# Diagonal score groups taken two at a time, and score windows put in the order of their due times, in a gated-attention and maxout kernel

## The chip, the cores and the metric

One NeuronCore of a Trainium2 chip runs the whole kernel. The metric is the device time of one execution in microseconds (us); lower is better. The core's engines work side by side and wait for one another through semaphores: TensorE (PE; its weight loads are listed as PEld), VectorE (DVE), ScalarE (ACT), GpSimd (POOL) and SyncE (SP). SP and POOL are used here mainly as queues that issue DMA transfers. Matmul results go to PSUM, which has eight banks; everything else lives in SBUF.

## The reference

```python
# u, v: 8 x 3072 x 256, z: 8 x 3072 x 64
scale  = 1.0 / S                                   # S = 3072
scores = scale * np.matmul(z, z.transpose(0, 2, 1))
attn   = np.maximum(scores, 0.0) ** 2
x      = (u * np.matmul(attn, v)).reshape(B * S, D)
h1, h2 = x @ w1, x @ w2                            # 256 -> 1024
out    = np.maximum(h1, h2) @ w_out                # 1024 -> 256
```

Eight sequences of 3072 rows go through an attention without softmax: the scores are z times its own transpose, so the score matrix is symmetric, and each score goes through relu and a square. The result times v is gated by u and goes through a two-branch layer whose branches are joined by a maximum. The types at the interface are float32; the kernel computes in bfloat16 with float32 accumulation.

## The kernel before

**Tiling.** A sequence is cut into 24 blocks of 128 rows, and four blocks make a group (`G = 4`, 512 rows). One *step* produces the output of one group, so there are 6 steps per sequence and 48 in all. A step accumulates, over all 24 blocks `k`, the block of v times the 128 x 512 score tile of block `k` against the group, into two PSUM accumulators `xacc` (two halves of the 256 features; line 262, recorded at the helper's line 74). That makes 48 matmuls of 512 columns. At the step's end two DVE operations (line 268) gate it with u and give `xT`. Three steps later (`LAG = 3`) `xT` goes through the maxout layer: `chunk_d` (tiles `d_ps`, then `g_sb`) and `chunk_o` (tiles `o_ps`, then `o_sb`, then the store).

**Scores and their symmetry.** Since the score matrix is symmetric, each tile is computed once, on or above the diagonal, and used twice: as it is in its own step (tile `a_sb`), and transposed in a later step (tile `aT`, filled by a DMA transpose on SP's queue, `turn`, lines 200 and 226). A score needs only 64 features, so a score matmul uses only 64 rows of the 128 x 128 array: `score` (line 190) puts it on the lower half (`j = 0`) or the upper half (`j = 1`), and two matmuls on different halves run at the same time. `scores_pair` (line 204) does two blocks: two 512-column matmuls on the two halves, into one PSUM tile of two banks; ACT takes relu into `r_sb` (line 218), DVE squares it into `a_sb` (line 221), and SP transposes it where the other triangle needs it.

**The diagonal.** In the diagonal group of a step (4 x 4 blocks) only the upper triangle is computed: `scores_diag` (line 234) does 4, 3, 2 and 1 blocks, which are matmuls of 512, 384, 256 and 128 columns on the halves 0, 1, 1, 0. The first two go to one PSUM tile, the others to a second one. ACT takes the relu of the first (line 246, 896 columns), DVE that of the second (line 248, 384 columns), DVE squares the four rows into `aD` (lines 249 to 252), and three `turn`s fill the lower triangle of `aD`. The first four steps of the first sequence do without this (`NDIAG`): they compute their whole diagonal as pairs. So there are 44 diagonals.

**The order.** TensorE's order is written out by hand: `work` is the list of its pieces (one block of a step for both accumulators is 432 ns by the list's own account), and `matmul` pins each instruction in the order of the program (line 73). SP's and POOL's DMAs are pinned too; ACT and DVE are ordered by the compiler's scheduler. Score tiles are grouped in *windows*, and each window is put between two pieces of `work`: all its score matmuls stand there in a row. In `before`, `tiles` lists the tiles of all steps in the order of the steps, a diagonal first and then the pairs (lines 498 to 501), and `windows` cuts that list: up to three PSUM tiles per window (`WIN = 3`), where a diagonal counts as two (its second is the entry `-1`), so that a diagonal shares its window with one pair. The three PSUM tiles are all that `mm_psum` has; the scores share them with `d_ps` and `o_ps`.

Each row of scores has a due time: the time of its first reader in `work` less an allowance, 2900 ns for a row of the step's own (`LAT_OWN`), 9000 for a transposed one (`LAT_TURNED`), 10000 for a diagonal (`LAT_DIAG`). Windows are laid from the last to the first, each at the latest allowed place (`spots`) that is not after the due time of any of its rows and at least `GAP` (2500 ns) before the next window:

```python
    for w in reversed(range(len(windows))):
        limit = min([limit] + [due[r] for r in windows[w] if r in due])
        found = [i for i in spots if begins[i] <= limit]
        i = found[-1] if found else 0
        laid.setdefault(i, []).insert(0, w)
        limit = begins[i] - (GAP if w > n_first else GAP_FIRST)
```

A place is allowed where no `chunk_d` or `chunk_o` piece lies within 860 ns before it and 1700 after it, since those use the same PSUM tiles.

**Buffers.** `NA`, `NT`, `ND` (line 51) are the numbers of `a_sb`, `aT` and `aD` tiles. Loads of u, v and z go through POOL's queue, each behind a one-column copy (`gate`, line 83) of the tile last written (`fresh`), which holds the load back until that tile exists.

Of the kernel before, what the change touches and what calls it, by code (L numbers as in the profile page):

```python
# [11 lines left out]
def kernel(  # L12
# [17 lines left out]
    nc = tc.nc  # L30
    fp32 = mybir.dt.float32
    bf16 = mybir.dt.bfloat16
    AF = mybir.ActivationFunctionType
    ALU = mybir.AluOpType

    B, S, D = u.shape
# [3 lines left out]
    P = 128  # L40
    NSB = S // P
    G = 4
    WIN = 3
    GW = G * P
    NG = NSB // G
# [2 lines left out]
    LAG = 3  # L48
    NDIR = 3
    NDIAG = 3  # L50
    NA, NT, ND = 18, 12, 3
    scale = 1.0 / S
    c2 = float(scale * scale)

# [7 lines left out]
    apool = ctx.enter_context(tc.tile_pool(name="apool", bufs=NA))  # L62
    dpool = ctx.enter_context(tc.tile_pool(name="dpool", bufs=ND))
# [4 lines left out]
    mm_psum = ctx.enter_context(tc.tile_pool(name="mm_psum", bufs=3, space=bass.MemoryType.PSUM))  # L68
# [4 lines left out]
    def matmul(*args, **kw):  # L73
        pin(nc.tensor.matmul(*args, **kw))  # L74

    def sp_dma(**kw):
        pin(nc.sync.dma_start(**kw))
# [108 lines left out]
    def direct(b, i, j):  # L186
        return b == 0 and i < j <= NDIR


    def score(q, out_ps, j, k, s, q0, n):  # L190
        half = ds(j * dqk, dqk)
        matmul(
            out_ps,
            q.zT[half, k + 1 - j, :],
            q.zT[half, ds(G * s + 1 - j + q0, n), :],
            start=True,
            stop=True,
        )

    def turn(out_ap, in_ap):  # L200
        sp_dma(out=out_ap, in_=in_ap, transpose=True)


    def scores_pair(b, s, k0):
        q = seqs[b]
        s_ps = mm_psum.tile([P, 2, GW], fp32, name="s_ps", tag="mm")
        for j in range(2):
            score(q, s_ps[:, j, :], j, k0 + j, s, 0, G)
        yield
        a_sb = apool.tile([P, 2, GW], bf16, name="a_sb")  # L210
        r_sb = apool.tile([P, 2, GW], bf16, name="r_sb", bufs=3)

        head = b == 0 and s == 0 and k0 < 10
        keep = pin if head else lambda ins: None
        if head and k0 in (2, 6):
            keep(nc.vector.tensor_single_scalar(out=r_sb, in_=s_ps, scalar=0.0, op=ALU.max))  # L216
        else:
            keep(nc.scalar.activation(r_sb, s_ps, AF.Relu))  # L218
        if head and k0 < 4:
            yield  # L220
        keep(nc.vector.tensor_mul(a_sb, r_sb, r_sb))  # L221
        gj = k0 // G
        if gj > s and not direct(b, s, gj):
            if (s, gj) not in q.T:
                q.T[s, gj] = tpool.tile([P, G, G, P], bf16, name="aT")
            turn(
                q.T[s, gj][:, ds(k0 - G * gj, 2), :, :].rearrange("p k q x -> p (k q) x"),
                a_sb.rearrange("p j q -> p (j q)"),
            )
        yield a_sb  # L230

    def scores_diag(b, s):
        q = seqs[b]
        k = G * s
        s_ps = mm_psum.tile([P, 2 * G, P], fp32, name="s_ps", tag="mm")
        s2_ps = mm_psum.tile([P, 2 * G, P], fp32, name="s2_ps", tag="mm")
        score(q, s_ps[:, 0:4, :], 0, k, s, 0, 4)
        score(q, s_ps[:, 4:7, :], 1, k + 1, s, 1, 3)  # L240
        score(q, s2_ps[:, 2:4, :], 1, k + 2, s, 2, 2)
        score(q, s2_ps[:, 4:5, :], 0, k + 3, s, 3, 1)
        yield
        aD = dpool.tile([P, G, G, P], bf16, name="aD")
        r_sb = apool.tile([P, 7, P], bf16, name="r_sb", bufs=3)
        nc.scalar.activation(r_sb, s_ps[:, 0:7, :], AF.Relu)  # L246
        r2_sb = apool.tile([P, 3, P], bf16, name="r2_sb", bufs=2)
        nc.vector.tensor_single_scalar(out=r2_sb, in_=s2_ps[:, 2:5, :], scalar=0.0, op=ALU.max)  # L248
        nc.vector.tensor_mul(aD[:, 0, :, :], r_sb[:, 0:4, :], r_sb[:, 0:4, :])
        nc.vector.tensor_mul(aD[:, 1, 1:4, :], r_sb[:, 4:7, :], r_sb[:, 4:7, :])  # L250
        nc.vector.tensor_mul(aD[:, 2, 2:4, :], r2_sb[:, 0:2, :], r2_sb[:, 0:2, :])
        nc.vector.tensor_mul(aD[:, 3, 3, :], r2_sb[:, 2, :], r2_sb[:, 2, :])
        for r in range(G - 1):
            turn(
                aD[:, r + 1 : G, r, :],
                aD[:, r, r + 1 : G, :].rearrange("p q x -> p (q x)"),
            )
        yield aD

    def attn(q, k, moving, xacc, dcs, first, last):  # L260
        for dc in dcs:
# [68 lines left out]
    q = seqs[0]  # L330
# [21 lines left out]
    fresh = [None]  # L352
# [61 lines left out]
    steps = [Step(b, s) for b in range(B) for s in range(NG)]  # L414
# [26 lines left out]
    for n, st in enumerate(steps):  # L441
        b, s = st.b, st.s
# [52 lines left out]
    put_o(last, True)  # L495


    tiles = []
    for n, st in enumerate(steps):
        for k0 in st.rows:  # L500
            tiles += [(n, None), (n, -1)] if k0 is None else [(n, k0)]
    windows, room = [], 0
    for i, (n, k0) in enumerate(tiles):
        if not room or (k0 is None and room < 2):
            windows.append([])
            room = 2 if i < 6 else WIN
        windows[-1].append((n, k0))
        room = 0 if (n + 1) % NG == 0 and k0 == -1 else room - 1

    begins, t = [], 0  # L510
    for ns, _, _, _ in work:
# [2 lines left out]
    due = {}  # L514
    for at, (_, _, _, reads) in zip(begins, work):
        for row, lat in reads if reads != "begin" else ():
            due[row] = min(due.get(row, t), at - lat)
    shared = [(at, at + w[0]) for at, w in zip(begins, work) if w[1]]

    def free(at):  # L520
# [13 lines left out]
        if free(at) and apart(at) and work[i][1] is False and work[i][0]  # L534
    ]
    GAP_FIRST, GAP = 2100, 2500
    n_first = sum(n < NG for n, _ in tiles) // WIN
    laid = {}
    limit = t
    for w in reversed(range(len(windows))):  # L540
# [3 lines that stand above are left out]
# [33 lines left out]
    for n, st in enumerate(steps):  # L577
        b, s = st.b, st.s
# [21 lines left out]
    transfers.sort()  # L600

    def scores_window(w):
        gens = []
        for n, k0 in windows[w]:
            st = steps[n]
            if k0 is None:
                gens.insert(0, (st, k0, scores_diag(st.b, st.s)))
            elif k0 >= 0:
                gens.append((st, k0, scores_pair(st.b, st.s, k0)))
        for st, k0, gen in gens:  # L610
            next(gen)
        for st, k0, gen in gens:
            st.scored[k0] = a = next(gen)
            fresh[0] = a[:, 0, 0:1] if k0 is not None else a[:, 0, 0, 0:1]


    steps[0].begin()
# [14 lines left out]
    gens = [scores_pair(0, 0, k0) for _, k0 in windows[0]]  # L632
# [12 lines left out]
    for i, (_, _, fn, _) in enumerate(work):  # L645
        for w in laid.get(i, []):
            scores_window(w)
        while transfers and transfers[0][0] <= begins[i]:
            _, _, is_load, begin_transfer = transfers.pop(0)
            if is_load:  # L650
                gate(fresh[0])
            begin_transfer()
        fn()
# [30 lines left out]
```

## Time and profile before

| what | value |
|---|---|
| median of 3 runs | 981.85 us (981.44 to 981.95) |
| the profiled execution, its own time | 981.29 us |
| span of the profiled execution | 979.5 us |
| granted TensorE clock | 1.00 over the span |
| PE matmuls on s_ps (scores) | 696 rows: 564 of 512 columns, 44 each of 384, 256 and 128 |
| mean of such a row | 380, 333, 269 and 216 ns |
| matmul rows on xacc, 512 columns | 379 ns |
| ACT relu, 1024 columns (L218) / 896 columns (L246) | 258 of 1023 ns / 44 of 917 ns |
| DVE relu of the diagonal's rest, 384 columns (L248) | 44 of 558 ns |
| DVE square of a pair, 1024 columns (L221) | 260 of 691 ns |
| DVE squares of a diagonal (L249 to L252) | 44 each of 425, 350, 292 and 218 ns |
| SP transposes aD / aT | 132 / 228, of 1.21 / 1.28 us each on the queue |
| the same, from issue to landing (lowest, median, longest) | 2.3, 2.4, 8.0 us / 3.1, 3.6, 10.6 us |
| DMA engines | hardware queue 61.5%, software queue 21.6% of 16 engines' span |

The profile's page gives, for the span of one execution, the busy time of each engine, the same in 40 equal slices (a digit is the busy share of a slice in tenths), and the chain of work that ended last, followed back from the last instruction. A line of a timeline has start, duration, engine, line of the code, operation, tiles (written <- read), shape and count; several equal instructions are drawn as one line. A line of the waits has the engine and tile that waited, what ended the wait, the total in us, how often, and the longest. A matmul's drawn duration is longer than the distance to the next matmul's start, because matmuls are pipelined: distances between starts tell what one costs. Some matmul records are missing in the trace, so counts on a matmul line can be a little short.

### The profile page before, as it was taken

Reading aid. Unit: us, or ns where it says so; the run is one execution under the profiler, and the core shown is the slowest. Engines: PE = TensorE matmul, PEld = TensorE weight load, DVE = VectorE, ACT = ScalarE, POOL = GpSimd, SP = SyncE. Lnnn points to the kernel's source line nnn. Section 1 sums busy time; section 2 is a strip of 40 time slices with the busy share of each in tenths; the row PEclk is TensorE's granted clock in tenths of the full one; section 3 lists DMA queues with packets and bytes.
Section 4 is the critical chain, followed back from the end, with each engine's and each line's share of the span. In section 5 each row is a group of like instructions: output and inputs, shape, how many; then the busy total and the mean of one; then the engine's idle time right before and its main releaser. Section 6 shows DMA issues by size and latency. Waiting matters only on the chain.

```text
span 979.5 us, 14514 instructions
## 1 busy us (share of the span) xinstructions
PE 968.7 (99%) x5662; PEld 510.3 (52%) x5743; DVE 432.2 (44%) x681; ACT 442.6 (45%) x500; POOL 77.7 (8%) x228
## 2 busy tenths in 40 slices
PE   9999999999999999999999999999999999999998
PEld 3355545555455554555545564455545555445556
DVE  6654444443544435433445334444345443554322
ACT  6853454334643355433554335533355433654322
POOL 2011000110001100010000100011000110000000
PEclk9999999999999999999999999999999999999999
DMA  9999599987999969897788979889778796796621
GB/s 151 171 161 187 103 182 150 164 149 123 175 160 144 155 123 177 150 170 128 151 156 144 179 119 157 148 153 181 135 147 149 136 187 127 149 161 118 109 66 65
DMA packets 378517, 143.46 MB, mean 146 GB/s; under 512 B 356944, under 2 KB 358608, under 8 KB 378448
## 3 DMA queue, kind: packets, MB, share of 16 engines
q1 hardware_dynamic: 361888, 112.78, 61.5%
q0 software_dynamic: 16560, 29.74, 21.6%
q8 instruction: 45, 0.74, 0.3%
q14 instruction: 24, 0.20, 0.1%
HBM read 59.77 MB, written 25.17 MB: 87 GB/s over the span
## 4 chain that ended last, share of the span: by engine, by line
PE 99%; issue 1%; DVE 0%; ACT 0%
PE xacc L74 52%; PE o_ps L74 21%; PE d_ps L74 17%; PE s_ps L74 8%; PE w2o_ps L74 0%; ACT r_sb L218 0%; DVE r_sb L216 0%; PE tpz L134 0%; DVE a_sb L221 0%; DVE o_sb L317 0%; DVE blank L333 0%
## 5 line engine op out<-in xcount | busy, mean ns | idle before, releaser
L74 PEld LDWEIGHTS <-v_sb 128*128 128x128 bf16 x2304 | 215.9, 98 | 277.7 <-issue 41.1
L218 ACT ACTIVATE r_sb<-s_ps 128x1024 bf16<-128x1024 f32 x258 | 248.6, 1023 | 111.4 <-PE s_ps L74 111.2
L221 DVE TENSOR_TENSOR a_sb<-r_sb 128x1024 bf16<-128x1024 bf16 x260 | 179.4, 691 | 212.9 <-ACT r_sb L218 208.9
L74 PE MATMUL xacc<-a_sb,v_sb 128*128 128x512 bf16 x997 | 231.3, 379 | 2.5 <-issue 0.2
L74 PE MATMUL xacc<-aT,v_sb 128*128 128x512 bf16 x912 | 216.5, 379 | 0.0
L74 PE MATMUL o_ps<-w_out_sb,g_sb 128*128 128x256 bf16 x1536 | 199.1, 273 | 0.0
L74 PE MATMUL d_ps<-xT,w_sb 128*128 128x512 bf16 x751 | 172.7, 379 | 0.9
L74 PEld LDWEIGHTS <-g_sb 128*128 128x128 bf16 x1536 | 149.9, 98 | 27.6
L292 ACT ACTIVATE g_sb<-d_ps 128x1024 bf16<-128x1024 f32 x96 | 98.3, 1024 | 138.8 <-PE d_ps L74 138.8
L292 DVE TENSOR_SCALAR g_sb<-d_ps 128x1024 bf16<-128x1024 f32 x96 | 117.4, 1223 | 84.7 <-PE d_ps L74 81.3
L323 ACT COPY o_sb<-o_ps 128x512 f32<-128x512 f32 x94 | 55.1, 586 | 178.2 <-PE o_ps L74 178.2
L268 DVE SCALAR_TENSOR_TENSOR xT<-xacc,uT 128x512 bf16<-128x512 f32 x96 | 62.0, 683 | 137.4 <-PE xacc L74 137.4
L74 PEld LDWEIGHTS <-w_sb 128*128 128x128 bf16 x768 | 75.1, 98 | 88.7
L74 PE MATMUL s_ps<-zT 64*128 64x512 bf16 (+3 forms) x696 | 89.2, 359 | 0.1
L246 ACT ACTIVATE r_sb<-s_ps 128x896 bf16<-128x896 f32 x44 | 40.3, 917 | 97.9 <-PE s_ps L74 97.9
L74 PE MATMUL xacc<-aD,v_sb 128*128 128x512 bf16 x331 | 79.9, 379 | 2.6 <-issue 2.2
L74 PE MATMUL o_ps<-W2o_sb,xT 128*128 128x256 bf16 x384 | 73.3, 273 | 0.0
L248 DVE TENSOR_SCALAR r_sb<-s_ps 128x384 bf16<-128x384 f32 x44 | 24.6, 558 | 95.3 <-PE s_ps L74 95.3
L74 PEld LDWEIGHTS <-zT 64*128 64x128 bf16 x696 | 27.3, 94 | 62.6 <-issue 50.5
L83 POOL COPY gate_sb<-g_sb 128x1 bf16<-128x1 bf16 x44 | 8.3, 188 | 407.8 <-DVE g_sb L292 238.5
L74 PEld LDWEIGHTS <-xT 128*128 128x128 bf16 x384 | 37.6, 98 | 4.3
L83 POOL COPY gate_sb<-a_sb 128x1 bf16<-128x1 bf16 x48 | 9.7, 202 | 271.8 <-DVE a_sb L221 271.8
(37 smaller groups left out, 143.3 us busy)
## 6 DMA issues: line engine op xcount, KB each, us to landing
out_dram<-o_sb SPq DMA_DIRECT2D x47, 512.0 KB, 4.1
v_sb<-in_v_dram POOLq DMA_DIRECT2D x48, 256.0 KB, 5.9
u_sb<-in_u_dram POOLq DMA_DIRECT2D x48, 256.0 KB, 5.3
aT<-a_sb SPq DMA_TRANSPOSE x228, 3.6
z_sb<-in_z_dram POOLq DMA_DIRECT2D x7, 384.0 KB, 7.5
aD<-aD SPq DMA_TRANSPOSE x132, 2.4
w_sb<-in_moe_w_dram POOLq DMA_DIRECT2D x2, 512.0 KB, 7.5
uT<-u_sb SPq DMA_TRANSPOSE x48, 4.3
```

The costliest lines, as they stand in the source:

```text
L74: pin(nc.tensor.matmul(*args, **kw))
L83: pin(nc.gpsimd.tensor_copy(gate_sb, tile_ap))
L218: keep(nc.scalar.activation(r_sb, s_ps, AF.Relu))
L221: keep(nc.vector.tensor_mul(a_sb, r_sb, r_sb))
L246: nc.scalar.activation(r_sb, s_ps[:, 0:7, :], AF.Relu)
L248: nc.vector.tensor_single_scalar(out=r2_sb, in_=s2_ps[:, 2:5, :], scalar=0.0, op=ALU.max)
L268: nc.vector.scalar_tensor_tensor(out=xT[:, dc, :].rearrange("p (t q) -> p t q", q=P), in0=xacc[dc].rearrange("p (t q) -> p t q", q=P), sca ...
L292: nc.any.tensor_single_scalar(out=g_sb[:, nb : nb + 2, :], in_=d_ps, scalar=0.0, op=ALU.max)
L323: nc.any.tensor_copy(o_sb[:, ds(2 * th, 2), :], o_ps[:, :, :D])
```

## The change

Two diagonals of neighbouring steps become one window, in three PSUM tiles instead of four: each has a tile for its rows of 4, 3 and 1 blocks (512, 384 and 128 columns on the halves 0, 1, 1; eight blocks, so the tile is full), and the two rows of 2 blocks share the third tile, one on each half and in a bank each. ACT takes the relu of each full tile (1024 columns), DVE that of the shared one in one operation (512 columns). A diagonal no longer stands with a pair.

The list of windows is made anew for each sequence: pairs in threes (the first six of the kernel in twos), diagonals in twos, and then all windows of the sequence are sorted by the earliest due time of their rows. The buffers become 13 `a_sb` (from 18), 13 `aT` (from 12) and 4 `aD` (from 3).

```diff
-    NA, NT, ND = 18, 12, 3
+    NA, NT, ND = 13, 13, 4
...
-    def scores_diag(b, s):
+    def scores_diags(b, ss):
         q = seqs[b]
-        k = G * s
-        s_ps = mm_psum.tile([P, 2 * G, P], fp32, name="s_ps", tag="mm")
-        s2_ps = mm_psum.tile([P, 2 * G, P], fp32, name="s2_ps", tag="mm")
-        score(q, s_ps[:, 0:4, :], 0, k, s, 0, 4)
-        score(q, s_ps[:, 4:7, :], 1, k + 1, s, 1, 3)
-        score(q, s2_ps[:, 2:4, :], 1, k + 2, s, 2, 2)
-        score(q, s2_ps[:, 4:5, :], 0, k + 3, s, 3, 1)
+        one = [mm_psum.tile([P, 2 * G, P], fp32, name="s_ps", tag="mm") for _ in ss]
+        two = mm_psum.tile([P, 2, G, P], fp32, name="s2_ps", tag="mm")
+        for s, s_ps in zip(ss, one):
+            k = G * s
+            score(q, s_ps[:, 0:4, :], 0, k, s, 0, 4)
+            score(q, s_ps[:, 4:7, :], 1, k + 1, s, 1, 3)
+            score(q, s_ps[:, 7:8, :], 1, k + 3, s, 3, 1)
+        for h, s in enumerate(ss):
+            score(q, two[:, h, 0:2, :], h, G * s + 2, s, 2, 2)
         yield
-        aD = dpool.tile([P, G, G, P], bf16, name="aD")
-        r_sb = apool.tile([P, 7, P], bf16, name="r_sb", bufs=3)
-        nc.scalar.activation(r_sb, s_ps[:, 0:7, :], AF.Relu)
-        r2_sb = apool.tile([P, 3, P], bf16, name="r2_sb", bufs=2)
-        nc.vector.tensor_single_scalar(out=r2_sb, in_=s2_ps[:, 2:5, :], scalar=0.0, op=ALU.max)
...
+        aDs = [dpool.tile([P, G, G, P], bf16, name="aD") for _ in ss]
+        r2_sb = apool.tile([P, 2, 2, P], bf16, name="r2_sb", bufs=2)
+        for h, s_ps in enumerate(one):
+            aD = aDs[h]
+            r_sb = apool.tile([P, 2 * G, P], bf16, name="r_sb", bufs=3)
+            nc.scalar.activation(r_sb, s_ps, AF.Relu)
+            if h == 0:
+                nc.vector.tensor_single_scalar(
+                    out=r2_sb, in_=two[:, :, 0:2, :], scalar=0.0, op=ALU.max
+                )
+            nc.vector.tensor_mul(aD[:, 0, :, :], r_sb[:, 0:4, :], r_sb[:, 0:4, :])
+            nc.vector.tensor_mul(aD[:, 1, 1:4, :], r_sb[:, 4:7, :], r_sb[:, 4:7, :])
+            nc.vector.tensor_mul(aD[:, 2, 2:4, :], r2_sb[:, h], r2_sb[:, h])
+            nc.vector.tensor_mul(aD[:, 3, 3, :], r_sb[:, 7, :], r_sb[:, 7, :])
+            for r in range(G - 1):
+                turn(
...
+        yield aDs
...
-    tiles = []
-    for n, st in enumerate(steps):
-        for k0 in st.rows:
-            tiles += [(n, None), (n, -1)] if k0 is None else [(n, k0)]
-    windows, room = [], 0
-    for i, (n, k0) in enumerate(tiles):
-        if not room or (k0 is None and room < 2):
-            windows.append([])
-            room = 2 if i < 6 else WIN
-        windows[-1].append((n, k0))
-        room = 0 if (n + 1) % NG == 0 and k0 == -1 else room - 1
...
+    windows = []
+    for b in range(B):
+        mine = [NG * b + s for s in range(NG)]
+        tiles = [(n, k0) for n in mine for k0 in steps[n].rows if k0 is not None]
+        part = [tiles[i : i + 2] for i in range(0, 6, 2)] if b == 0 else []
+        tiles = tiles[sum(map(len, part)) :]
+        part += [tiles[i : i + WIN] for i in range(0, len(tiles), WIN)]
+        diags = [n for n in mine if steps[n].diag]
+        part += [[(n, None) for n in diags[i : i + 2]] for i in range(0, len(diags), 2)]
+        windows += sorted(part, key=lambda w: min(due[r] for r in w))
...
     def scores_window(w):
-        gens = []
-        for n, k0 in windows[w]:
-            st = steps[n]
-            if k0 is None:
-                gens.insert(0, (st, k0, scores_diag(st.b, st.s)))
-            elif k0 >= 0:
-                gens.append((st, k0, scores_pair(st.b, st.s, k0)))
+        rows = windows[w]
+        b = steps[rows[0][0]].b
+        if rows[0][1] is None:
+            gen = scores_diags(b, [steps[n].s for n, _ in rows])
+            next(gen)
+            for (n, _), a in zip(rows, next(gen)):
+                steps[n].scored[None] = a
+                fresh[0] = a[:, 0, 0, 0:1]
+            return
+        gens = [(steps[n], k0, scores_pair(b, steps[n].s, k0)) for n, k0 in rows]
```

More of the change, by code (lines that the diff above doesn't have):

```diff
@@ L230, in scores_pair @@
         yield a_sb
-    def scores_diag(b, s):
+    def scores_diags(b, ss):
         q = seqs[b]
-        k = G * s
-        s_ps = mm_psum.tile([P, 2 * G, P], fp32, name="s_ps", tag="mm")
-        s2_ps = mm_psum.tile([P, 2 * G, P], fp32, name="s2_ps", tag="mm")
-        score(q, s_ps[:, 0:4, :], 0, k, s, 0, 4)
-        score(q, s_ps[:, 4:7, :], 1, k + 1, s, 1, 3)
-        score(q, s2_ps[:, 2:4, :], 1, k + 2, s, 2, 2)
-        score(q, s2_ps[:, 4:5, :], 0, k + 3, s, 3, 1)
-        yield
-        aD = dpool.tile([P, G, G, P], bf16, name="aD")
-        r_sb = apool.tile([P, 7, P], bf16, name="r_sb", bufs=3)
-        nc.scalar.activation(r_sb, s_ps[:, 0:7, :], AF.Relu)
-        r2_sb = apool.tile([P, 3, P], bf16, name="r2_sb", bufs=2)
-        nc.vector.tensor_single_scalar(out=r2_sb, in_=s2_ps[:, 2:5, :], scalar=0.0, op=ALU.max)
[L249 to L258, printed above, removed]
@@ new lines, in scores_diags @@
+        aDs = [dpool.tile([P, G, G, P], bf16, name="aD") for _ in ss]
[14 more added lines that the diff above has]
+                turn(
+                    aD[:, r + 1 : G, r, :],
+                    aD[:, r, r + 1 : G, :].rearrange("p q x -> p (q x)"),
+                )
@@ L536 @@
     GAP_FIRST, GAP = 2100, 2500
-    n_first = sum(n < NG for n, _ in tiles) // WIN
+    n_first = sum(w[0][0] < NG for w in windows)
     laid = {}
@@ L613, in scores_window @@
             st.scored[k0] = a = next(gen)
-            fresh[0] = a[:, 0, 0:1] if k0 is not None else a[:, 0, 0, 0:1]
+            fresh[0] = a[:, 0, 0:1]
     steps[0].begin()
```

## The prediction

> **What bounds the kernel now.** I read the page first: engine totals, slices, and the chain that ended last.
>
> ```profile
> span 979.5 us, 14514 instructions
> PE 968.7 (99%) x5662; PEld 510.3 (52%) x5743; DVE 432.2 (44%) x681; ACT 442.6 (45%) x500; POOL 77.7 (8%) x228
> ...
> PE   9999999999999999999999999999999999999998
> ...
> PE 99%; issue 1%; DVE 0%; ACT 0%
> ```
>
> TensorE is busy in every slice and the chain of waits never leaves it. A busy row does not yet exclude pauses under 1%, so I next read the waits of PE:
>
> ```profile
> PEld L74 <- issue: 92.7, 244, 0.4
> ...
> PE xacc L74 <- issue: 2.4, 15, 0.2
> ```
>
> After the start-up, PE waits for no engine and no DMA. What is left is "issue", at most 0.4 us at a time, and the timeline shows what that is:
>
> ```profile
> 23.74 2.76 PE L74 MATMUL xacc<-a_sb,v_sb 128*128 128x512 bf16 x12
> 26.43 0.82 PE L74 MATMUL s_ps<-zT 64*128 64x512 bf16 x6
> 27.19 2.76 PE L74 MATMUL xacc<-a_sb,v_sb 128*128 128x512 bf16 x12
> 29.88 0.82 PE L74 MATMUL s_ps<-zT 64*128 64x512 bf16 x6
> ```
>
> Twelve 512-column matmuls in 2.76 us, the last drawn 0.379 long, start (2.76 - 0.379)/11 = 0.216 us apart. From 23.74 to 26.43 are 2.69 us: eleven steps of 0.216 and one of 0.312. So going from the full array to the two half-array (64-row) score matmuls costs 0.096 us. The last score pair of a window starts 0.308 us before the next full matmul (single starts in the trace), 0.092 over its own 0.216: the way back. **Every score window therefore costs PE two turnovers, 0.188 us, besides its columns.** The window with a diagonal:
>
> ```profile
> 77.74 1.03 PE L74 MATMUL xacc<-aT,v_sb 128*128 128x512 bf16 x4
> 78.70 0.66 PE L74 MATMUL s_ps<-zT 64*128 64x512 bf16 x6
> 79.29 0.60 PE L74 MATMUL xacc<-aT,v_sb 128*128 128x512 bf16 x2
> ```
>
> Its six matmuls are 512, 384, 256, 128 columns of a diagonal and 512, 512 of a pair; single starts in the trace are 78.701, .704, .877, .927, .983, .986, then 79.294. The three kinds of window, from first score matmul to next full matmul plus 0.096: three pairs 0.754 + 0.096 = 0.850 (70 of them), diagonal and pair 0.594 + 0.096 = 0.690 (44), two pairs 0.538 + 0.096 = 0.634 (3). Together 59.50 + 30.36 + 1.90 = 91.76 us.
>
> **The change on PE.** The instruction order of the changed program has 110 runs of score matmuls where 117 stood: 84 of three pairs, 4 of two, 22 of two diagonals (512, 384, 128, 512, 384, 128, 256, 256). The number of matmuls, their columns and all others are the same. Call the lower half A (512, 512, 256) and the upper B (384, 128, 384, 128, 256). Gaps from the trace: 384 columns to the next on the same half 0.173; 128 columns to the next 0.056; 512 to the next 0.226 the first time in a window, 0.216 then; starts keep the program's order. A512 at 0; B384 0.003; B128 0.176; A512 0.226; B384 at 0.176 + 0.056 = 0.232; B128 0.163 to 0.173 after it, 0.395 to 0.405; A256 0.442; B256 between 0.445 (A sets it) and 0.461 (B sets it). Then its 256 columns (0.109) and the way back (0.092): 0.646 to 0.662. I take 0.652, with the turnover in 0.748.
>
> Sum: 84 x 0.850 + 22 x 0.748 + 4 x 0.634 = 71.40 + 16.46 + 2.54 = 90.39. **Change -1.37 us**, with the two ends of the new window -1.50 and -1.15. Nearly all is seven windows fewer at 0.188 (1.32 us); the packing of the columns itself gives next to nothing.
>
> A rule speaks against it. The Trainium skill, "TensorE: Matmul & The Clock Gate", Part 3, says that a weight load overlaps running matmuls only when it goes to another row group. The row first: 384 columns and then 256 on the same half started 0.173 apart, 0.162 being the 384 columns alone, so that load was covered here. By the rule half B would go as in the third rival below, and the sum would be +6.6 instead of -1.37. The row decides.
>
> **The other engines, costed at nothing.** ACT: 44 activations grow from 917 to 1023 ns, +4.7 us on an engine busy 45%. DVE: 44 of 558 ns become 22 of 512 columns, by the line from 384 (558) to 1024 (1222) some 691 ns: 24.6 falls to 15.2 us. The multiplies are the same (425, 350, 292, 218). DMA: the same 132 aD and 228 aT transposes, reordered. The cover of all this is the lead that a window has over its first reader. For pairs:
>
> ```profile
> 300.59 0.82 PE L74 MATMUL s_ps<-zT 64*128 64x512 bf16 x6
> ...
> 301.02 2.85 ACT L218 ACTIVATE r_sb<-s_ps 128x1024 bf16<-128x1024 f32 x3 [2.76 <-PE s_ps L74]
> ...
> 302.08 0.69 DVE L221 TENSOR_TENSOR a_sb<-r_sb 128x1024 bf16<-128x1024 bf16 x1 [2.75 <-ACT r_sb L218]
> ...
> 303.91 0.69 DVE L221 TENSOR_TENSOR a_sb<-r_sb 128x1024 bf16<-128x1024 bf16 x1 [0.23 <-ACT r_sb L218]
> ```
>
> The first pair is ready 2.18 us after the window's start, the third 4.01. The planner puts a window 2.9 us ahead of its first own row (LAT_OWN), and rows in due order are read 0.86 us per pair: third 2.9 + 1.73 - 4.01 = 0.6 us spare, which is positive without help from other slack. In the trace of before the smallest steady spare was 0.42 (at 150.7). Should ACT be held by one g_sb of 1.02 us, 0.4 us would show on PE, once. Turned tiles (aT) landed at least 12.8 us before their first matmul, so the queue's new order has that to spend. a_sb buffers fall from 18 to 13: at one window of three pairs per 3.45 us, the densest stretch (above), a buffer is wanted again after 13/3 x 3.45 = 14.9 us, while its multiply ends 4 us after the window's start at the latest and its transpose landed within 10.6 (3.6 in the median). PSUM: a new window takes three tiles as one of three pairs does, and gives them back sooner (two activations and one DVE operation, not three activations in line). If any of these runs out, its engine's next PSUM eviction is late, then a score window on PE.
>
> **Where the new order could bite: the diagonal of step 4 in each sequence.** Before:
>
> ```profile
> 198.52 0.66 PE L74 MATMUL s_ps<-zT 64*128 64x512 bf16 x6
> ...
> 200.35 3.74 SPq L77 DMA_TRANSPOSE aD<-aD  x3
> ...
> 205.55 3.87 SPq L77 DMA_TRANSPOSE aD<-aD  x3
> ...
> 211.10 1.89 PE L74 MATMUL xacc<-aD,v_sb 128*128 128x512 bf16 x8
> ```
>
> The turns go out 1.83 us after the window's start, 1.26 apart; the third landed at 205.26, 5.6 us before the weight load of the first reader (210.87). Now the window stands two pieces of 0.43 later (199.38), its ACT row is 0.11 longer: first turn near 201.3, third near 203.85. Two windows in front of the reader (2 x 0.690) become one (0.748): the reader comes at 210.24. Behind these three turns SP now holds three of step 5, wanted a step later (979.5/48 = 20.4 us), and then the output store (issued at 210.86 before). POOL's next loads are gated by the window's last tile, as before (204.79 then, near 205 now). Turns landed in 2.3 to 8.0 us, median 2.4: at 2.4 the reader has 4.0 us to spare, at 6.56 (the turn of 205.55) it is 0.2 late, at 8.0 1.6 late. I take the median, to which most rows are near.
>
> **Sum.** The profiled execution took 981.29 (span 979.5), so 979.9 for one like it; it lies 0.56 under the median of the three runs, 981.85. Against that median: 980.5 us. My case's own range is 979.9 (981.44 - 1.50) to 980.8 (981.95 - 1.15).
>
> **Rivals.**
> Late turns, slower: at step 4's diagonal of seven sequences the third turn falls into the v loads issued at 205.38 and 206.02 and lands after 8.0 us. Price 7 x 1.6 = 11.2 - 1.4: 991.7; it beats the gain by 0.2% from 0.5 us late in each, a turn of 6.9 us or more. For: the turn at 205.55 took 6.56. Against: the new third turn goes out 1.5 us before that load, and the aT turn issued at 204.20 landed in 3.1. Chance 0.11.
> More gain, faster: the idle of the weight loads ("issue" 41.1 us before v_sb and 50.5 before zT) is what windows really cost, 91.6/117 = 0.78 each; seven fewer give 5.5: 976.4. Against: start-to-start gaps account for the period of 3.45 us with 0.188. Scatter of the runs with the upper end of my gain also counts here. Chance 0.12.
> Half B in line with its own weight loads, so that the packed window is dearer (slower too): a zT load (94 ns in the page's row) after the columns at each of B's four successions puts B256 at 0.003 + 2 x (0.162 + 0.094) + 2 x (0.056 + 0.094) = 0.815 instead of 0.451, 0.364 longer; 22 x 0.364 - 1.4 = +6.6: 988.5. Against: the 0.173 above. Chance 0.03.
> That the change does less than it says (order alone, no packing: each 512 waits for the one before and nothing of B hides, 0.662) is the upper end of my own case.
>
> **Chances.** My case 0.74. A measurement of this kernel tells about 0.2% (1.96 us) from no change; my gain of 0.14% lies inside. Within: 0.69 of my case and 0.01 of late turns, 0.70. Faster: 0.05 of mine by scatter and 0.12, 0.17. Slower: 0.10 and 0.03, 0.13. Range 979.5 (the low end with 0.4 of scatter) to 982.5 (the turns 0.3 us late in each of seven), which leaves out about 2 in 10.
>
> **What would show it.** 110 score windows; windows of eight matmuls lasting 0.65 us to the next full matmul; no wait of PE for DVE, ACT or DMA beyond the first 20 us; a span near 978.2; ACT busy some 5 us more, DVE some 9 less. I am wrong if PE shows waits on aD transposes, or if the gap between the second B384 and its B128 exceeds 0.2 us.

## The result, and the profile after

The changed kernel took 988.46 us in the median of 14 executions (981.03 to 1000.02); the kernel before, run beside it, took 981.92 (981.44 to 993.08, 14 executions). The ratio is 1.0051 (95% interval 1.0026 to 1.0076; executions more than 1.5% above the fastest of their kernel are left out of ratios, which therefore understate the loss, while the medians and counts given here take all). The change made the kernel slower, by 0.5% in that ratio and 6.5 us in the medians, where 980.5 and "the same" had been predicted.

The distribution tells more than the median. The fastest execution, 981.03, is below every one of before beside it, and it is the one that was profiled; but 13 of 14 lie above 983 us. So the profile shows the gain and only the beginning of the loss. Its page, engine totals and chain of waits:

```profile
span 979.3 us, 14613 instructions
PE 968.0 (99%) x5662; PEld 510.8 (52%) x5743; DVE 416.3 (43%) x659; ACT 446.6 (46%) x500; POOL 77.9 (8%) x228
...
PE 97%; DMA 1%; issue 1%; DVE 0%; ACT 0%
PE xacc L74 51%; PE o_ps L74 21%; PE d_ps L74 17%; PE s_ps L74 8%; DMA aD<-aD 1%; PE w2o_ps L74 0%; ACT r_sb L218 0%; DVE r_sb L216 0%; PE tpz L134 0%; ACT r_sb L252 0%; DVE aD L257 0%; DVE a_sb L221 0%; DVE aD L258 0%; DVE o_sb L325 0%; DVE aD L259 0%
```

The second line of the chain, shares by line, has an entry that before did not have: DMA aD, the transposes of the diagonal. The waits of PE and of its weight loads name it too (who waited, what ended it, total us, times, longest):

```profile
PE xacc L74 <- DMA aD<-aD: 0.4, 1, 0.4
...
PEld L74 <- DMA aD<-aD: 1.2, 2, 0.9
```

It is a small wait, at one place, in step 4 of the seventh sequence. In the timeline of after:

```profile
802.39 8.12 SPq L77 DMA_TRANSPOSE aD<-aD  x6
...
803.44 0.19 POOL L83 COPY gate_sb<-aD 128x1 bf16<-128x1 bf16 x1 [3.08 <-DVE aD L257]
...
803.89 0.53 POOL L86 DMA_DIRECT2D v_sb<-in_v_dram  x1 [0.26 <-issue]
...
804.53 0.53 POOL L86 DMA_DIRECT2D v_sb<-in_v_dram  x1
...
812.96 1.04 PE L74 MATMUL xacc<-aD,v_sb 128*128 128x512 bf16 x4 [0.42 <-DMA aD<-aD]
```

The three turns that the reader needs went out at 802.39, 803.75 and 805.04 and landed at 809.14, 812.91 and 813.27: 6.8 to 9.2 us each, where the median of all aD turns is 2.4. Two v loads of 256 KB were issued between them and landed at 811.43 and 812.73. That is the place and the mechanism of the prediction's rival "late turns".

**The spare time of the step-4 turns** (from the landing of the last of the three to the weight load of the first matmul that reads the tile; the block that the third turn fills is read only 1.3 us later, so a spare just below zero need not show as a wait) was, in the seven steady sequences of the two profiled executions:

| | 2nd | 3rd | 4th | 5th | 6th | 7th | 8th |
|---|---|---|---|---|---|---|---|
| before, us | 5.62 | 3.30 | 5.68 | 5.01 | 5.59 | 5.02 | 5.63 |
| after, us | 1.43 | -0.53 | 1.28 | 0.89 | 1.64 | -1.97 | 4.04 |

From the second sequence on every other aD tile had at least 13 us in after, and PE waited for no aT tile; in the first sequence the tile of step 4 had 3.4 us, where it had 3.1 before. The eighth has no later sequence to load for, and there the 4.0 us that the prediction worked out are what was measured.

How the loads moved is read from the second sequence. After:

```profile
202.16 7.69 SPq L77 DMA_TRANSPOSE aD<-aD  x6
...
203.21 0.19 POOL L83 COPY gate_sb<-aD 128x1 bf16<-128x1 bf16 x1 [3.08 <-DVE aD L257]
...
203.66 0.53 POOL L86 DMA_DIRECT2D v_sb<-in_v_dram  x1 [0.26 <-issue]
```

and before:

```profile
200.35 3.74 SPq L77 DMA_TRANSPOSE aD<-aD  x3
...
204.93 0.19 POOL L83 COPY gate_sb<-a_sb 128x1 bf16<-128x1 bf16 x1 [5.64 <-DVE a_sb L221]
...
205.38 0.53 POOL L86 DMA_DIRECT2D v_sb<-in_v_dram  x1 [0.26 <-issue]
```

Before, the load's gate copied the pair's `a_sb`, written last in the window, 4.6 us after the first turn went out. In after a diagonal window has no pair. The tile that gates is the first square of the second diagonal (`fresh` takes `a[:, 0, 0, 0:1]`), 1.05 us after the first turn. The turns went out 1.8 us later than before and the loads 1.7 us earlier: they now start in the middle of the turns.

Something else changed that the prediction had not looked at, the stretch ahead of the turns. Busy time by stretches of 10 us; the last two columns are the busy share of the DMA engines (which can exceed 1) and GB/s. Before, then after:

```profile
170.00:180.00 10.00, 9.95 (x49) 4.39 (x49) 6.02 (x10) 3.88 (x4) 1.16 (x4) 1.00 0.70 127
180.00:190.00 10.00, 9.95 (x68) 6.19 (x68) 2.08 (x3) 4.03 (x5) 1.64 (x5) 1.00 1.12 165
190.00:200.00 10.00, 10.00 (x51) 4.40 (x50) 4.69 (x7) 3.10 (x4) 1.44 (x4) 1.00 1.15 214
```

```profile
170.00:180.00 10.00, 9.95 (x50) 4.22 (x49) 5.61 (x7) 4.90 (x5) 0.70 (x2) 1.00 1.19 208
180.00:190.00 10.00, 9.95 (x69) 6.21 (x69) 2.08 (x3) 4.03 (x5) 2.10 (x7) 1.00 1.19 172
190.00:200.00 10.00, 10.00 (x48) 4.48 (x46) 3.74 (x4) 2.05 (x2) 1.31 (x4) 1.00 1.18 237
```

Before had a lull (0.70) before the diagonal's turns; after has none. Pairs cut in threes put two pairs of step 4 into one window with the last of step 3, and the whole window takes the earliest due time of its rows. Their two aT turns, issued at 204.20 and 209.51 before, go out at 187.34 and 188.68 now: between 165 and 192 us SP issues nine aT turns where it issued four.

### The profile page after: what moved, and what is told of

Same layout as the page of the kernel before. It is cut to its first block, busy times and chain, and to the rows that moved or that the text cites. A ratio compares the mean times of both kernels' runs of the same rounds, so it can differ in the third digit from the quotient of the medians.

```text
span 979.3 us, 14613 instructions
## 1 busy us (share of the span) xinstructions
PE 968.0 (99%) x5662; PEld 510.8 (52%) x5743; DVE 416.3 (43%) x659; ACT 446.6 (46%) x500; POOL 77.9 (8%) x228
## 4 chain that ended last, share of the span: by engine, by line
PE 97%; DMA 1%; issue 1%; DVE 0%; ACT 0%
PE xacc L74 51%; PE o_ps L74 21%; PE d_ps L74 17%; PE s_ps L74 8%; DMA aD<-aD 1%; PE w2o_ps L74 0%; ACT r_sb L218 0%; DVE r_sb L216 0%; PE tpz L134 0%; ACT r_sb L252 0%; DVE aD L257 0%; DVE a_sb L221 0%; DVE aD L258 0%; DVE o_sb L325 0%; DVE aD L259 0%
## 5 line engine op out<-in xcount | busy, mean ns | idle before, releaser
L218 ACT ACTIVATE r_sb<-s_ps 128x1024 bf16<-128x1024 f32 x258 | 245.8, 1024 | 162.4 <-PE s_ps L74 162.2
L300 ACT ACTIVATE g_sb<-d_ps 128x1024 bf16<-128x1024 f32 x96 | 98.3, 1024 | 133.3 <-PE d_ps L74 133.3
L252 ACT ACTIVATE r_sb<-s_ps 128x1024 bf16<-128x1024 f32 x44 | 42.6, 1021 | 42.2 <-PE s_ps L74 42.2
L254 DVE TENSOR_SCALAR r_sb<-s_ps 128x512 bf16<-128x512 f32 x22 | 15.2, 692 | 28.2 <-PE s_ps L74 28.2
L86 POOL DMA_DIRECT2D u_sb<-in_u_dram x48 | 25.6, 534 | 17.8 <-issue 17.8
```

Source lines behind the costliest of these rows:

```text
L86: pin(nc.gpsimd.dma_start(**kw))
L254: nc.vector.tensor_single_scalar(out=r2_sb, in_=two[:, :, 0:2, :], scalar=0.0, op=ALU.max)
L300: nc.any.tensor_single_scalar(out=g_sb[:, nb : nb + 2, :], in_=d_ps, scalar=0.0, op=ALU.max)
```

## The experiments

The theories: **loads**, the v loads are released too early by the new gate and run beside the turns; **lead**, the diagonal window merely stands too near its reader; **queue**, the stretch of 30 us ahead of the turns is now so full that a disturbance there isn't worked off before the turns; **buffers**, fewer `a_sb` tiles or the new order of the windows make other waits. All kernels compute the whole reference.

**The control.** The changed kernel again, beside three variants on the same chip.

> The changed kernel once more, as the control on the same chip. All theories: times scattered between 981 and 1000 us, median about 986 to 990; in the profile PE waits on aD transposes at the diagonal of step 4 of a sequence (near 211 us and every 120 us after).

985.73 us (981.32 to 1010.08; 8 of 10 above 983), before 982.05 (981.13 to 994.07), ratio 1.0007 (0.9969 to 1.0046). The profiled execution was one of the bad ones, 1010.08 with a span of 1008.3, and shows what a bad one is made of. The waits of PE:

```profile
PE xacc L74 <- DMA aD<-aD: 21.6, 3, 8.8
```

Three stalls make 21.6 us, in the second, third and seventh sequence. The first of them on the timeline, by SP's queue, POOL's first v load and PE:

```profile
184.46 11.11 SPq L77 DMA_TRANSPOSE aT<-a_sb  x3
...
197.15 8.48 SPq L77 DMA_TRANSPOSE zT<-z_sb  x2
...
203.26 0.53 POOL L86 DMA_DIRECT2D v_sb<-in_v_dram  x1 [0.26 <-issue]
...
205.72 7.97 SPq L77 DMA_TRANSPOSE uT<-u_sb  x1
...
213.79 7.72 SPq L77 DMA_TRANSPOSE aD<-aD  x6
...
220.25 2.74 PE L74 MATMUL xacc<-aD,v_sb 128*128 128x512 bf16 x6 [8.76 <-DMA aD<-aD]
```

The first `aD` square was ready at 201.7, but SP could not issue its turn before 213.79, 3 us after its reader was due: the aT, zT and uT transposes ahead of it held the queue for 11.1, 8.5 and 8.0 us, where the good execution held it for 8.3, 5.0 and 1.3. The turns themselves then took 4.5 to 6.4 us. The two v loads, released by the `aD` square, went out at 203.26 and 203.90, some 10 us ahead of the turns, and landed at 217.41 and 218.62. And the stall is paid a second time, on the clock (third column from the right, the granted clock):

```profile
216.00:220.00 4.00, 0.00 (x0) 0.00 (x0) 0.00 (x0) 0.00 (x0) 0.00 (x0) 0.50 1.29 151
...
221.00:223.00 2.00, 2.00 (x6) 0.76 (x5) 0.40 (x1) 0.00 (x0) 0.00 (x0) 0.50 0.28 96
223.00:226.00 3.00, 3.00 (x8) 1.06 (x7) 0.89 (x2) 1.02 (x1) 0.00 (x0) 0.50 0.82 209
```

From 215.9 to 226.2 the clock was 0.50, the last 5.9 us of it with PE at work again. Over the three stalls (10.2, 10.2 and 6.8 us at half clock, of which PE worked 5.9, 5.3 and 4.8) half of that work time, some 8.0 us, is lost: 21.6 + 8.0 = 29.6, and 1008.3 - 29.6 = 978.7, near the 979.3 of the good execution. So in this execution the late turns account for the whole excess, and the buffers theory falls: after the start-up PE waited for nothing else.

**The gate alone undone:** after a diagonal window the loads are gated by the first diagonal's last turned block, so they can't start before the turns have landed.

```diff
-                fresh[0] = a[:, 0, 0, 0:1]
+            fresh[0] = steps[rows[0][0]].scored[None][:, G - 1, G - 2, 0:1]
```

> The changed kernel, with the loads that follow a diagonal window gated by the last turned block of the window's first diagonal instead of by its first square, so that they are issued only when the three turns of step 4 have landed. Loads theory (the turns land late because two v loads go out between them): the third turn lands 2.3 to 3.5 us after its issue, the smallest spare of an aD tile rises from about -2 to +1.6 us to 3 to 4.5 us, no wait of PE on aD, time 980.2 to 980.8 us with a scatter under 1 us. Lead theory (the turns go out too late, whatever the loads do): no change, 984 to 1000 us. Buffer theory (fewer a_sb tiles or the order of the windows make other waits): no change.

982.91 us (980.25 to 996.58; 5 of 10 above 983), ratio 1.0002 (0.9970 to 1.0034). The last turn landed 2.3 to 3.3 us after its issue, and in six of the seven sequences the spare was 2.3 to 4.1, so the loads were what made the turns slow in good executions. But the scatter stayed. In the profile the spare of the fifth sequence is -1.3 us, still without a wait: zT held SP from 558.85 for 6.84 us, uT for 3.55, and the first aD turn went out at 569.42. The one wait for aD, 1.4 us, is in the first sequence, where zT held SP up to 86.51 and the turns went out from 86.60 on. The loads theory explains a part; 5 late executions of 10 against the control's 8 are too few to say how much.

**More lead.** The diagonal's allowance 3 us longer; since places for windows are coarse, the window of step 4 in the second sequence moved 7.8 us further ahead of its reader.

```diff
-    LAT_OWN, LAT_TURNED, LAT_DIAG = 2900, 9000, 10000
+    LAT_OWN, LAT_TURNED, LAT_DIAG = 2900, 9000, 13000
```

> The changed kernel with 3 us more allowance for a diagonal (LAT_DIAG 13000 for 10000), so that diagonal windows stand earlier; the gates are unchanged. Loads theory: the loads follow the earlier tile and still meet the turns, which take 4 to 9 us, but the reader comes 5 to 6 us later after them than before: no or rare waits, 980.3 to 982 us. Lead theory: the turns land in 2.4 us far ahead of the reader, 980.4 us. Buffer theory: no change, 984 to 1000 us.

983.61 us (980.34 to 990.31; 6 of 10 above 983), ratio 1.0008 (0.9973 to 1.0043). The profiled execution (span 987.7) has one wait of 5.0 us for aD, with the clock at 0.5 from 216.3 on for 6.8 us: the first turn, issued at 203.18 right behind two zT transposes, took 15.7 us. Lead of this size does not cure it: the window stood at 194.49, but aT and zT transposes held SP up to 203.08, and by then v loads hung on `g_sb` and went out at 201.48, 202.84 and 203.49, so the turns still met them.

**The gate one step further:** windows of diagonals leave the gate alone (the line `fresh[0] = a[:, 0, 0, 0:1]` is taken out), so the loads are gated by the tile written before it (`g_sb` in the trace) and start ahead of the turns.

> The changed kernel, with the diagonals no longer gating the loads: the two v loads hang on the g_sb tile before and go out some 2.5 us earlier, ahead of the first turn instead of between the turns. Loads theory: the turns queue behind the loads and land when these land, but that is 2.5 us earlier than in the changed kernel: spare of aD about 2.5 us more (0.5 to 4 us), fewer waits, 980.5 to 985 us. Lead theory and buffer theory: no change, 984 to 1000 us.

The 4 executions took 981.0, 991.99, 996.27 and 1005.26 us. I had expected fewer waits; there were more (two waits for aD, 8.5 us, in a profile of 990.2). Loads that go out ahead of the turns are no better than loads beside them; with 4 executions more can't be said.

**The loads taken out of the way,** in the changed kernel and in the one before: the v loads of all sequences but the first move from steps 3 and 4 to step 5.

```diff
-                v_at = [(3, 2), (3, 8), (3, 14), (4, 2), (4, 8), (4, 14)]
+                v_at = [(5, 14), (5, 1), (5, 4), (5, 7), (5, 10), (5, 12)]
```

> The changed kernel with all six v loads of the next sequence moved from steps 3 and 4 to step 5 (sequences 1 to 7; the first sequence's plan is left). Queue theory (in steps 3 and 4 the DMA engines have more than they can do, so that step 4's diagonal turns go out late or land late): without the v loads the DMA share from 170 to 205 us falls under 1, the turns land 2.3 to 3 us after issue, the spare of step 4's aD is 3.5 to 4.2 us in every sequence but the first, clock 1.0, times 980.2 to 981 us nearly always. Lead theory (10 us of allowance are too few after the two diagonals were joined, whatever else is on the queues): spare stays under 2 us, 984 to 1000 us. Scatter of the chip alone: outliers as before, 3 or 4 in 10.

> The kernel before, with the same move of the v loads to step 5. All theories: clean runs as before, 981.2 to 982 us. Queue theory: the rare outliers of the kernel before (4 of 39 executions over 985 us) go too.

In the changed kernel: 980.51 us (979.89 to 998.10; 2 of 10 above 983), before 981.90 (981.28 to 997.04), ratio 0.9990 (0.9970 to 1.0010). In the kernel before: 981.59 (981.15 to 982.31, none above 983), ratio 0.9990 (0.9976 to 1.0005). The difference of the two, with the loads in the same place, is what the change itself brings: -1.08 us in the medians, -1.26 between the fastest. The spare is 3.2 to 4.1 us, so the lead theory, which had it under 2, fails here; the 2 late executions of 10 are not clear of the 5 of 31 that the kernel before had beside them. The profile of the changed kernel with late loads, its chain and its waits of PE:

```profile
PE 98%; issue 1%; DMA 0%; DVE 0%; ACT 0%
```

```profile
PE xacc L74 <- issue: 2.4, 15, 0.2
PE xacc L74 <- DVE blank L341: 1.2, 1, 1.2
```

No wait for aD is left, and the stretch has room from 180 on:

```profile
180.00:190.00 10.00, 9.95 (x69) 6.22 (x69) 2.43 (x4) 4.03 (x5) 0.72 (x2) 1.00 0.97 170
190.00:200.00 10.00, 10.00 (x48) 4.58 (x47) 3.74 (x4) 2.05 (x2) 0.19 (x1) 1.00 0.86 162
200.00:210.00 10.00, 10.00 (x72) 6.36 (x71) 2.66 (x9) 3.11 (x4) 0.53 (x1) 1.00 0.35 62
```

**Much more lead:** `LAT_DIAG` 22000.

> The changed kernel with an allowance of 22 us for a diagonal (LAT_DIAG 22000 for 10000): step 4's diagonal window stands a step earlier, at the start of step 3, before the z transposes on SP's queue. Queue theory: the aD waits go (spare over 15 us), but what is left in the queue is as much as before, so that at most other transposes (uT, aT, zT) are late in some executions: 980.3 to 983 us. Lead theory: the waits go altogether, 980.4 us without outliers.

983.04 us (981.31 to 987.49; 5 of 10 above 983), ratio 1.0017 (1.0003 to 1.0030). The aD turns had 17 us or more and nothing waited for them, yet it is slower than before: its fastest is 1.4 us above that of the late loads. In the profile other pauses came up, near 54 us one of PE of 0.4 us and one of 0.8 us for `xT`, behind a u transpose for which DVE had waited 14.8 us. The lead theory, that distance alone cures it, falls.

**The pairs of step 4 in a window of their own,** as the old cut had them; the diagonal window, its gate's tile and its packing stay.

```diff
-        part += [tiles[i : i + WIN] for i in range(0, len(tiles), WIN)]
+        for cut in [t for t in tiles if t[0] % NG < 4], [t for t in tiles if t[0] % NG >= 4]:
+            part += [cut[i : i + WIN] for i in range(0, len(cut), WIN)]
```

> The changed kernel with step 4's two pairs in a window of their own, as late as their due time allows, instead of in one window with the last pair of step 3 (seven to eight windows more: +1.3 to 1.5 us, so 981.6 to 982 us when nothing is late). Queue theory: two aT turns of 1.28 us leave the full stretch from 170 to 200 us, so its DMA share falls to about that of the kernel before (1.0 to 1.1) and outliers are fewer than in the changed kernel, 981.6 to 985 us. Lead theory: the diagonal's place is nearly the same, so the scatter is as in the changed kernel, median 985 to 990 us.

982.15 us (981.51 to 990.08; 4 of 10 above 983), ratio 1.0018 (0.9996 to 1.0040). A window of pairs now follows the diagonal and gates the loads, and the spare is back at 4.0 to 5.6 us. But in the second sequence the stretch is as full as in after (0.95, 1.13, 1.16, 1.23 from 160 to 200; over six sequences 1.06 for 1.16), and late executions remain. The windows that it adds also cost the gain: its fastest time is 981.51, where before had 981.28 beside it.

**The early loads alone, in the kernel before:** windows with a diagonal don't gate loads.

```diff
-            fresh[0] = a[:, 0, 0:1] if k0 is not None else a[:, 0, 0, 0:1]
+            if all(r is not None for _, r in windows[w]):
+                fresh[0] = a[:, 0, 0:1]
```

> The kernel before (no pairing of diagonals, old order), with one line changed: a window that holds a diagonal no longer gates the loads, so that the two v loads of step 4 go out some 4 us earlier, between the turns of step 4's diagonal. Queue theory: the old kernel becomes unsteady as the changed one is: spare of step 4's aD from 5.6 down to 1 to 3 us, turns of 4 to 8 us, median 983 to 990 us. Lead theory (the allowance and the joined window are what hurts): no change, 981.2 to 982 us with an outlier or so.

981.72 us (981.24 to 986.46; 1 of 10 above 983), ratio 1.0000 (0.9990 to 1.0009). I had expected a median of 983 to 990, and that was wrong: the spare did fall as far as in after (1.0 to 2.5 us in four sequences, -0.2 and -3.7 in two), but in 9 of 10 executions that was enough. What the old order kept was the lull, 0.61 between 170 and 180. Its profiled execution was its one late one, with a wait of 2.5 us for aD.

**Only the queue relieved.** The z load of the next sequence and its zT transposes go out some 25 us earlier; the gate and the v loads stay as in the changed kernel.

```diff
-                z_at, zT_at = (2, 9), (3, 12)
+                z_at, zT_at = (1, 6), (2, 2)
```

> The changed kernel with the z load and its zT transposes issued some 25 us earlier, out of the stretch 190-200 us where the a-transposes, zT, uT and the step-4 turns all go out on SP's queue; gates and v loads stay as in the changed kernel. Theory 'two causes' (v loads 1.7 us early AND a DMA stretch 170-200 us that is full): the spare of the step-4 turns in an undisturbed execution stays near 1.4 us, because the v loads still go out beside the turns, but the turns are issued no later than their window asks, so few executions leave 980-983; median 981-983. Theory 'loads alone': nothing changes, median 983-988 with the same scatter up to about 1000. Theory 'queue alone': spare back to 4 us and median 980-981.

980.81 us (979.73 to 990.59; 2 of 10 above 983), ratio 0.9998 (0.9960 to 1.0036). The spare stayed small, 0.2 to 1.6 us and once -1.1, for the loads still run beside the turns. Yet 8 of 10 executions came down to 979.7 to 982.3. "Loads alone" falls, and "queue alone" too, since the spare did not come back. This holds if the changed kernel, which was not run beside it, scatters there as it did elsewhere; the kernel before had 2 of 13 above 983 beside it.

**The best version.** Late v loads and `LAT_DIAG` 13000; in the second kernel the first sequence's v loads are late too.

> The changed kernel with the v loads of sequences 1 to 7 in step 5 and 13 us of allowance for a diagonal: both causes of a thin spare taken away. Queue theory: spare of step 4's aD 8 to 11 us, no wait of PE on a DMA, lowest 979.9 us, median 980.3 us, outliers rarer than the 2 in 10 of the run with the v loads alone; against the kernel before 0.9986. If outliers stay as frequent, they are not the diagonals' and something else is late in those executions.

> The same, with the first sequence's v loads (for the second sequence) moved to step 5 as well. Queue theory: as the run beside it, with the spare at 91 us (3.7 us in the profile so far) raised as the others are; if the outliers came from the first sequence they go: median 980.3 us, all executions under 983 us.

The first: 981.03 us (980.14 to 982.26, and one execution of 1993.34, which I can't explain), ratio 0.9987 (0.9977 to 0.9996). The second: 980.94 (980.07 to 982.91, all 11 below 983), before 982.17 (981.14 to 984.09), ratio 0.9988 (0.9979 to 0.9997). Both beat the kernel before, by 0.13% and 0.12%, and in both the interval excludes no change. The medians are some 0.7 us above the 980.3 expected; the spare was 5.1 to 11.8 us.

**The runs together.** The share is the mean over the 30 us ahead of the step-4 turns of sequences 2 to 7 (170 to 200, 290 to 320 and so on); the spare is the median of the seven. Both come from one profiled execution of each kernel, a late one (above 983 us) in the four rows marked so.

| kernel | DMA share | spare, us | above 983 us |
|---|---|---|---|
| before | 0.96 | 5.6 | 13 of 110 |
| before, v loads later | 0.79 | 5.6 | 0 of 10 |
| before, early loads (late) | 1.00 | 1.3 | 1 of 10 |
| after | 1.16 | 1.3 | 21 of 24 |
| gate behind the turns | 1.17 | 3.6 | 5 of 10 |
| 3 us more lead (late) | 1.10 | 4.2 | 6 of 10 |
| gate one step further (late) | 1.10 | -0.1 | 3 of 4 |
| lead of 22 us (late) | 1.08 | 23.7 | 5 of 10 |
| step 4 split | 1.06 | 5.5 | 4 of 10 |
| z and zT earlier | 1.10 | 0.8 | 2 of 10 |
| v loads later | 1.00 | 4.0 | 2 of 10 |
| v loads later, 3 us more lead | 1.06 | 11.5 | 1 of 11 |
| all v later, 3 us more lead | 1.09 | 11.7 | 0 of 11 |

The changed kernel has the small spare and the full stretch together, and is late most often. A small spare alone did little harm (before with early loads), a full stretch alone some (gate behind the turns). But the share does not order the counts: from 1.06 to 1.10 they go from 0 of 11 to 6 of 10. How the harm divides is not settled with 10 executions of each, all the less as the changed kernel was run beside three of its variants only, the two with the gate moved and the one with 3 us more lead; the others ran on other chips than the control, beside the kernel before, which had 2 to 5 late executions each time. Why one execution works the same transfers off and another doesn't also stays open.

## Why the prediction was wrong

**TensorE's sum: right.** A window of two diagonals lasts 0.65 us to the next full matmul, as predicted (0.652):

```profile
79.09 0.72 PE L74 MATMUL s_ps<-zT 64*128 64x512 bf16 x8
79.74 2.33 PE L74 MATMUL xacc<-aT,v_sb 128*128 128x512 bf16 x10
```

The start-up differs between executions by up to 1 us, so spans are best compared from the first real matmul. Before and with late loads:

```profile
8.18 1.02 PE L74 MATMUL xacc<-a_sb,v_sb 128*128 128x512 bf16 x4
```

```profile
9.01 1.02 PE L74 MATMUL xacc<-a_sb,v_sb 128*128 128x512 bf16 x4
```

979.5 - 8.18 = 971.32 and 978.9 - 9.01 = 969.89: -1.43 us, where -1.37 was the sum. Two more profiles give the same lengths to 0.05 us (before with late loads, and late loads with 3 us more lead). The rivals "more gain" and "half B in line with its own weight loads" fall with it: the latter would have made the window 1.02 us.

**ACT and DVE: right and hidden.** ACT is up 4.0 us (predicted 4.7). On DVE the relu of the diagonals fell from 24.6 to 15.2 as predicted; the engine's total fell by 15.9, more than the groups' sum. No wait for either was added. PSUM and the `a_sb` buffers held.

**When the turns go out: right.** The first turn was predicted at 201.3 and came at 202.16, the third at 203.85 and came at 204.72. The window and the reader were 0.83 us later than predicted too (reader 211.07 for 210.24), 0.38 of it from the profile's later start-up, so the distances are as predicted.

**The step that failed** is the sentence "POOL's next loads are gated by the window's last tile, as before (204.79 then, near 205 now)". The gate's tile is not the last of the window any more; it is the second diagonal's first square, written at 203.1, and the first load went out at 203.66. The argument drawn from it, "the new third turn goes out 1.5 us before that load", is reversed: the third turn went out 1.06 us after it. This stood in the diff, in the lines on `fresh`, and would have been found by asking of the load what was asked of the turns.

**The second failure is the price.** "I take the median, to which most rows are near": 2.4 us is the median over 132 turns, and only 21 of them are these. In after the third turn took 4.5 to 8.2 us in the six sequences that load for a next one, and the spare, put at 4.0 us, was 0.9 to 1.6 in four of them and below zero in two. The trace of before had a sign of it: the first turn of step 5, issued 0.1 to 0.5 us behind a v load (205.55 behind 205.38), took 5.9 to 8.0 us in all six of these sequences, and 2.4 in the eighth, which has no later one to load for. In after the step-4 turns stand in that place.

The new order of the aT turns was costed at nothing because they had time to spare. They did; but the stretch ahead of the turns became full, and in the control SP was held until 213.79. The prediction's own case had no term for turns that go out late, nor for the clock after a stall: in the control's profile these are the 21.6 us of waits and some 8.0 us of half clock. Waits of PE for aD transposes were the prediction's own sign of being wrong.

**The rival "late turns"** named the right place, mechanism and direction, at a chance of 0.11. Its price (7 x 1.6 us) assumed the same small lateness in each sequence. In the profiled late executions of the changed kernel and its variants most sequences are in time and one to three stall, for up to 8.8 us; and part of that is paid twice, as half clock. That its 991.7 is near the measured 988.46 is partly luck.

## What to carry to other kernels

When a change regroups work, ask of each load what tile releases it: the gate moves with the grouping even where no line of the load changes. Price a transfer by the stretch in which it runs and by the spare to its reader, not by the median of its kind; work that is moved "for free" into a lull can take the room in which a later transfer would catch up. And where the fastest execution gains and the median loses, look at a bad execution: here the gain of 1.4 us was real, and moving loads that had no hurry brought it out.

## What the runs showed of the hardware

- After five stalls of PE of 5.0 to 8.8 us (the control, 3 us more lead, the gate one step further) the granted clock went to 0.50 for 6.8 or 10.2 us, beginning 2.3 to 4.5 us after PE fell idle and lasting 3.9 to 5.9 us on into the work; the loss is some 8.0 us in the control's profile. After a stall of 2.5 us (before with early loads) it was 0.50 for 3.4 us, from 0.4 us after PE had started again. Pauses of 1.6 us and less showed none of this.
- A turn of the diagonal (one to three blocks of 128 x 128) landed in 2.3 us at the quickest, but in after most of the step-4 turns took 4 to 9 us where 256 KB loads were in flight, and landed near them. SP itself was held by a single transpose for up to 8.0 us (uT in the control).
- A stretch with more DMA busy time can move less: from 200 to 210 us the bad execution had a share of 1.34 at 105 GB/s, the good one (after) 0.93 at 144. Identical programs differ in this from execution to execution; the kernel before has it too (13 of 110 above 983 us).
